# Attention with two gated layers on one core: the sums' guard on ScalarE, the first pair without GpSimd, small work with a choice of engine, and a new planned order

## The chip, the core and the metric

The kernel runs on one core of a Trainium2 chip. The metric is the device time of one execution in microseconds (us); what is compared is the median of several runs. Profiles are taken of one execution. The core has five engines that run side by side, each working through its own instructions in the order in which they were written: TensorE (PE in the profile; PEld is its weight load), VectorE (DVE), ScalarE (ACT), GpSimd (POOL) and SyncE (SP), which here issues nearly all transfers between memory and the core.

## The reference

```python
def _attn_ref(q, k, v):                     # q, k, v: 4 x 8 heads x 576 x 64
    q_rot, k_rot = (rotate(q), rotate(k))   # rotary embedding, cos and sin tables
    scores = scale * np.matmul(q_rot, k_rot.transpose(0, 1, 3, 2))
    scores = scores - np.max(scores, axis=-1, keepdims=True)
    attn = np.exp(scores)
    attn = attn / (np.sum(attn, axis=-1, keepdims=True) + 1e-09)
    return np.matmul(attn, v).astype(np.float32)

def _moe_ref(x, w_gate, w_val, w_out):      # 2304 tokens x 512, 1536 wide
    g = x @ w_gate
    silu = g * (1.0 / (1.0 + np.exp(-g)))
    return (silu * (x @ w_val) @ w_out).astype(np.float32)

def _moe2_ref(x, w_in, w_out):              # 2304 tokens x 512, 2048 wide
    r = np.maximum(x @ w_in, 0.0)
    return (r * r @ w_out).astype(np.float32)

# reference: _moe2_ref(_moe_ref(_attn_ref(q, k, v) as tokens x 512))
```

The `1e-09` that is added to the sums of the softmax is what the text calls the guard.

## The kernel before

The work falls into two stages. The first is attention, in 16 pairs of heads (4 blocks of the batch, 4 pairs each). The second holds the two gated layers and is one long run of matmuls. Each fp32 operand is split into a high and a low part in the fp32r format, and a product is made of three matmuls: high by high, high by low, low by high.

In the first stage nothing runs in the order in which it stands in the code. The functions `add_prep`, `add_kq`, `add_scores`, `add_values`, `add_spill`, `add_weight` and `add_filler` hand small operations to a `Plan`: the engine (or several to choose from, `add_any`), a time in ns that the planner takes for it, what it reads and writes, and a rank. `Plan.order()` then goes through a clock of its own: whenever an engine is free it takes the ready operation of lowest rank, and an operation with several engines goes to the first that takes it. The resulting order is written out, and each engine works through its share of it in that order, waiting on semaphores. The ranks come from the tables `RANK`, `RANK0` (first block) and `RANK1` (first two pairs); `FIRST` orders the first pair. `HOPS` holds times from engine to engine, `SWITCH` what a return of TensorE from transposes (mode 1) to products (mode 0) is taken to cost, `STAY` what is added to the rank of the other mode.

For each pair: q and k come in with the rotated halves beside them (tile `rot`); rope is a multiplication by the tables `cs` (or `csq`, which is `cs` times 0.125) and an addition of both halves (lines 487 and 488, on GpSimd, for pair 1 on GpSimd or VectorE). ScalarE makes the high part (line 531), GpSimd the low one (line 533), and SyncE copies both into the tiles `kh`, `qa` and `qz` by DMA (line 545). TensorE makes the scores `s` (line 565, two PSUM places), VectorE their maximum (571), ScalarE the exponential with its sum (573) into `p`. TensorE transposes `p` (594, two PSUM places `pt`), ScalarE or VectorE copies the result out (586, 588), TensorE multiplies by v (628, 631).

The sums are treated so: GpSimd adds the guard (line 637 for four columns, twice in a pair; line 600 for the ninth, once), VectorE takes the reciprocal (638, 601), ScalarE broadcasts it to `rb` (639), TensorE transposes `rb` (649) and VectorE multiplies (651). A normalised tile is split by ScalarE (657) and GpSimd (659). Pair 0 is different: rope on VectorE straight from the loads (481, 483), high parts by ScalarE (515, 521), low parts by VectorE (516, 522), and `qz` is a GpSimd copy of `qa` (525). The table `csq` is made by ScalarE (736).

Fillers are matmuls of the first gated layer for blocks 0 to 2 and its first two chunks of weights (line 704); they are planned into the attention stage with ranks of their own, and their weights are unpacked there (lines 226 to 231).

Of the kernel before, what the change touches and what calls it, by code (L numbers as in the profile page):

```python
# [12 lines left out]
AF = mybir.ActivationFunctionType  # L13
# [10 lines left out]
RANK0 = dict(ld=-0.835, rope=-50.984, k=29.955, lo=-87.1, dup=32.08, v=-8.825, s=-140.07, mx=-104.755, ex=-124.918, pt=-62.05, hi=246.519, av=23.841, rec=-40.109, x=-103.798, out=-29.73, fin=-99.107, scale=7.973)  # L24
RANK1 = dict(ld=53.997, rope=-27.634, k=14.826, lo=-66.302, dup=-17.819, v=-47.75, s=-62.932, mx=-81.823, ex=-200.205, pt=-33.078, hi=39.408, av=-5.906, rec=93.306, x=-80.138, out=-32.589, fin=-39.784, scale=-29.722)
# [22 lines left out]
class Plan:  # L48
# [9 lines left out]
    SWITCH = 80  # L58
    STAY = 67.654
# [4 lines left out]

    LAND = 2000
    RATE = 350

    def add(self, eng, ns, fn, rd=(), wr=(), rank=0.0, hold=0, mode=0, port=False, size=0, claim=()):
        self.add_any([(eng, ns, fn)], rd, wr, rank, hold, mode, port, size, claim)

    def add_any(self, ways, rd=(), wr=(), rank=0.0, hold=0, mode=0, port=False, size=0, claim=()):
# [18 lines left out]
        self.ops.append(dict(ways=ways, eng=ways[0][0], ns=ways[0][1], fn=ways[0][2], deps=deps, bufs=bufs, rank=(round(rank, 6), i), hold=hold, mode=mode, port=port, size=size))  # L90

    def order(self):
# [10 lines left out]
        busy, mode = {}, {}  # L103
        moved = 0.0
# [15 lines left out]
        out = []  # L120
        while events:
# [23 lines left out]
            for eng, heaps in ready.items():  # L145
                while any(heaps) and not busy.get(eng):
# [35 lines left out]
def tile_attention_moe_moe2(  # L182
# [161 lines left out]
    with ExitStack() as p1:  # L344
# [114 lines left out]
        def add_prep(g):  # L459
# [5 lines left out]
            for n, (c0, c1) in enumerate(parts(g)):  # L465
# [7 lines left out]
                for i in (1, 0):  # L473
                    x = P["rot"][i]
                    if g == 0:

                        at0 = FIRST["rope"][n][i]
                        y = buf("pt", [128, 512], bufs=2, pool=pp) if i else buf(("av", "mm")[n], [128, 512], pool=pp)
                        for e in range(2):
                            o = (lambda x=x, c0=c0, c1=c1: x()[:, 0, c0:c1]) if e == 0 else (lambda y=y, w=w: y()[:, :w])  # L480
                            plan.add("DVE", dve(w, 150), lambda x=x, o=o, c0=c0, c1=c1, e=e: nc.vector.tensor_tensor(out=o(), in0=x()[:, e, c0:c1], in1=cs()[:, e, c0:c1], op=ALU.mult),
                                     [(cs, n)] + ([] if e == 0 else [(x, n)]), [(x, n)] if e == 0 else [y], at0, port=True)
                        plan.add("DVE", dve(w, 150), lambda x=x, y=y, w=w, c0=c0, c1=c1: nc.vector.tensor_tensor(out=y()[:, :w], in0=y()[:, :w], in1=x()[:, 0, c0:c1], op=ALU.add), [(x, n)], [y], at0)
                        P[i, n] = (y, lambda y=y, w=w: y()[:, :w])
                        continue
# [4 lines left out]
                    for cols, fn in steps:  # L490
# [3 lines left out]
                        plan.add_any(ways, csk if i else [csq], [(x, n)], at + 0.01 * (1 - i), port=True)  # L494
# [6 lines left out]
        def add_kq(g):  # L501
# [5 lines left out]
            if g == 0:  # L507
                for n, (c0, c1) in enumerate(PARTS):
                    w, c = c1 - c0, slice(c0, c1)
                    (yk, kx), (yq, qx) = P[1, n], P[0, n]  # L510
                    for h in range(2):
                        own, other = rowsof(h)
                        at = FIRST["k"][n][h]
                        for r, p in ((own, 0), (other, 1)):
                            plan.add("ACT", act(w, 190), lambda h=h, own=own, r=r, c=c, kx=kx: nc.scalar.activation(kh()[r, h, c], kx()[own], AF.Copy), [yk], [(kh, (h, p, n))], at)
# [3 lines left out]
                        for (c, qc), (_, zc) in zip(q_at(h, c0, c1, NR), q_at(h, c0, c1, 0)):  # L519
# [5 lines left out]
                            plan.add("Pool", 550, lambda own=own, qc=qc, zc=zc: nc.gpsimd.tensor_copy(qz()[own, zc], raw(qa()[own, qc])), [(qa, (h, 0, n))], [(qz, (h, n))], at)  # L525
# [11 lines left out]
            for h in range(2):  # L537
# [6 lines left out]
                for (key, src), c, dst, wr, late in moves:  # L544
                    plan.add("SP", 450, lambda src=src, own=own, c=c, dst=dst: nc.sync.dma_start(out=raw(dst()), in_=src()[own, c]), [key], wr, at + 0.005 * late, size=256 * (c.stop - c.start))  # L545

        def add_scores(g):
# [4 lines left out]
            for x in range(NT):  # L552
# [3 lines left out]
                for i in range(2):  # L556
# [13 lines left out]
                    plan.add("PE", pe(HS) * (2 if t < 4 else 3), mm, rd, [ps], at + rk("s", g))  # L570
# [6 lines left out]
        def add_values(g):  # L577
# [22 lines left out]
            plan.add("Pool", 110, lambda: nc.gpsimd.tensor_scalar(rr(), sums()[:, 8:9], 1e-9, None, ALU.add), [(sums, 8)], [rr], at)  # L600
# [4 lines left out]
            for i in range(2):  # L605
# [3 lines left out]
                for c in range(5):  # L609
                    at = start + c * 0.08  # L610
                    pt = buf("pt", [128, 512], bufs=2, pool=pp)
                    plan.add("PE", 4 * 110, lambda c=c, pt=pt, tiles=tiles, pcs=pcs: (pcs[c](), transposes(tiles, c, pt, 0)), tiles, [pt], at + rk("pt", g), mode=1, claim=[pcs[c]])
                    copy(pt, pcs[c], 512, 128 if c < 4 else NR, at + rk("hi", g), [pcs[c]])
                rdr = []
                if i:
                    pcr = pcr_of()
                    for n in range(2):
                        at = start + (5 + n) * 0.08
                        pt = buf("pt", [128, 512], bufs=2, pool=pp)
                        plan.add("PE", (4 - 3 * n) * 110, lambda n=n, pt=pt, pcr=pcr: [pcr()] + [transposes([pr], c, pt, 128 * (c % 4)) for c in (range(4), (4,))[n]], [pr], [pt], at + rk("pt", g), mode=1, claim=[pcr])  # L620
# [11 lines left out]
                plan.add("PE", 5 * 420 + 300 + 600 * i, mm, pcs + rdr + [(vt, 0), (vt, 1)], [av], start + 0.45 + rk("av", g), mode=1)  # L632
# [265 lines left out]
```

## Time and profile before

| what | value |
|---|---|
| median of 3 runs | 1152.36 us (1151.9 to 1153.92) |
| the profiled execution | 1151.21 us, its span 1149.4 us |
| busy share of the span | TensorE 97%, VectorE 50%, ScalarE 42%, GpSimd 42% |
| chain that ended last, by engine | PE 77%, POOL 8%, DMA 5%, DVE 3%, SPq 2%, ACT 2%, issue 2% |
| mean granted clock of TensorE | 0.997 |

The span goes from the first to the last instruction of the profiled execution; the time of the run has a little more around it. A wait is given as the idle time of an engine in front of an instruction, with the instruction that ended the wait behind an arrow. A busy TensorE is not a TensorE at its peak, as matmuls overlap and their ends are modelled; what counts below is when it stood still.

### The profile page before, as it was taken

The numbers are of one execution on the slowest core, as the hardware profiler recorded it, in microseconds if no ns is written. First come the engines' busy times: TensorE is split into PE (matmuls) and PEld (weight loads), VectorE is DVE, ScalarE is ACT, GpSimd is POOL, SyncE is SP. The second block draws the span as 40 slices with busy tenths as digits, with TensorE's granted clock in tenths as the row PEclk, the third lists the DMA queues.
The fourth block names the chain that finished last, engine by engine and source line by source line (L and its number), as shares of the span: only waits on it lengthen the run. The fifth ranks groups of instructions, "written<-read, shape, count | busy, mean of one in ns | idle before, by whom it ended". The sixth has DMA issues, their size and how long they took to land.

```text
span 1149.4 us, 16627 instructions
## 1 busy us (share of the span) xinstructions
PE 1110.1 (97%) x6336; PEld 929.5 (81%) x6336; DVE 574.4 (50%) x953; ACT 477.6 (42%) x970; POOL 487.2 (42%) x417
## 2 busy tenths in 40 slices
PE   4898999999999999999999999999999999999998
PEld 3686877788888888888888888888888888888886
DVE  7676765766673655537346274461153236233222
ACT  6666766676663433213132132443352224223121
POOL 6887666576214433214132144562243234224121
PEclk9999999999999999999999999999999999999999
DMA  9765655646327522103011020120031012000112
GB/s 297 214 186 170 170 171 161 185 135 176 79 75 261 206 74 73 39 4 107 1 56 55 1 92 19 37 74 1 1 105 42 1 48 81 1 1 1 67 26 74
DMA packets 61104, 102.44 MB, mean 89 GB/s; under 512 B 11104, under 2 KB 37216, under 8 KB 60128
## 3 DMA queue, kind: packets, MB, share of 16 engines
q1 hardware_dynamic: 59904, 96.59, 28.0%
q0 software_dynamic: 576, 4.19, 1.0%
q8 instruction: 50, 0.82, 0.3%
q10 hardware_dynamic: 544, 0.59, 0.2%
q14 instruction: 30, 0.25, 0.1%
HBM read 67.17 MB, written 12.06 MB: 69 GB/s over the span
## 4 chain that ended last, share of the span: by engine, by line
PE 77%; POOL 8%; DMA 5%; DVE 3%; SPq 2%; ACT 2%; issue 2%; POOLq 0%; DVEq 0%; ACTq 0%
PE mm L267 22%; PE mm L268 22%; PE mm L269 22%; PE s L565 3%; PE pt L594 3%; POOL rot L487 3%; PE av L628 3%; PE mm L704 2%; SPq L545 2%; POOL rot L488 1%; DMA rot<-in_k_dram 1%; DMA qa<-rot 1%; DMA v<-in_v_dram 1%; DMA rot<-in_q_dram 1%; POOL kl L533 1%
## 5 line engine op out<-in xcount | busy, mean ns | idle before, releaser
L282 POOL TENSOR_TENSOR h<-s,h 128x512 fp32r<-128x512 f32 (+1 forms) x80 | 96.2, 1202 | 182.1 <-ACT h L281 182.1
L282 POOL TENSOR_TENSOR h<-hf,h 128x512 fp32r<-128x512 f32 (+1 forms) x54 | 66.8, 1237 | 151.6 <-ACT h L281 148.9
L301 DVE TENSOR_TENSOR s<-r,mm 128x512 f32<-128x512 f32 (+1 forms) x80 | 50.6, 632 | 147.0 <-POOL h L282 75.4
L571 DVE TENSOR_REDUCE nm<-s 128x1 f32<-128x576 f32 x144 | 104.6, 749 | 21.2 <-PE s L565 20.1
L573 ACT ACTIVATE p<-s,nm 128x576 f32<-128x576 f32 x144 | 105.7, 737 | 20.3 <-DVE nm L571 18.7
L565 PE MATMUL s<-kh,qa 128*128 128x288 f32 x320 | 94.0, 326 | 18.8 <-DVE qa L522 10.8
L594 PE MATMUL pt<-ident,p 128*128 128x128 f32 (+1 forms) x720 | 101.4, 279 | 10.4 <-DVE pc L588 6.6
L268 PE MATMUL mm<-wo,h 128*128 128x512 f32 x288 | 110.8, 389 | 0.0
L267 PE MATMUL mm<-wo,h 128*128 128x512 f32 x288 | 109.5, 389 | 0.0
L594 PEld LDWEIGHTS pt<-ident,p 128*128 128x128 f32 (+1 forms) x720 | 82.6, 137 | 23.4 <-DVE pc L588 8.4
L269 PE MATMUL mm<-wo,h 128*128 128x512 f32 x288 | 93.2, 389 | 0.0
L299 ACT ACTIVATE r<-mm 128x512 f32<-128x512 f32 (+1 forms) x80 | 43.9, 549 | 118.5 <-PE mm L269 118.1
L231 POOL TENSOR_TENSOR wi<-wa,wi 128x512 fp32r<-128x512 f32 x36 | 47.2, 1310 | 108.3 <-ACT wi L230 108.3
L290 DVE SCALAR_TENSOR_TENSOR th<-th,mm 128x512 f32<-128x512 f32 (+1 forms) x54 | 33.8, 626 | 107.2 <-ACT th L288 107.2
L565 PE MATMUL s<-kl,qz 128*128 128x288 f32 x288 | 83.0, 305 | 1.6 <-POOL qz L525 1.6
L228 DVE SCALAR_TENSOR_TENSOR wp<-wa,wp 128x512 uint32<-128x512 uint32 x62 | 53.4, 862 | 58.4 <-ACT wa L226 58.4
L565 PEld LDWEIGHTS s<-kh,qa 128*128 128x128 f32 x320 | 60.9, 196 | 25.9 <-ACT p L573 13.3
L281 ACT ACTIVATE h<-s 128x512 fp32r<-128x512 f32 (+1 forms) x80 | 47.2, 589 | 78.2 <-DVE s L301 78.2
L628 PE MATMUL av<-pc,v 128*64 128x256 f32 x640 | 76.8, 387 | 0.0
L269 PE MATMUL mm<-h,wo 128*128 128x512 f32 (+1 forms) x200 | 72.6, 369 | 0.0
L281 ACT ACTIVATE h<-hf 128x512 fp32r<-128x512 f32 (+1 forms) x54 | 31.5, 583 | 98.9 <-DVE hf L293 98.4
L268 PE MATMUL mm<-h,wo 128*128 128x512 f32 (+1 forms) x200 | 72.6, 368 | 0.0
(212 smaller groups left out, 2794.7 us busy)
## 6 DMA issues: line engine op xcount, KB each, us to landing
raw<-in_moe_w_out_dram SPq DMA_DIRECT2D x26, 512.0 KB, 3.5
rot<-in_k_dram SPq DMA_DIRECT2D x15, 576.0 KB, 4.2
rot<-in_q_dram SPq DMA_DIRECT2D x15, 576.0 KB, 3.8
kh<-rot SPq DMA_DIRECT2D x60, 144.0 KB, 2.6
raw<-in_moe_w_in_dram SPq DMA_DIRECT2D x16, 512.0 KB, 3.6
raw<-in_moe_w_gate_dram SPq DMA_DIRECT2D x10, 512.0 KB, 3.6
raw<-in_moe_w_val_dram SPq DMA_DIRECT2D x10, 512.0 KB, 3.7
qa<-rot SPq DMA_DIRECT2D x30, 144.0 KB, 2.6
```

Source lines behind the costliest of these rows:

```text
L228: lambda: nc.vector.scalar_tensor_tensor(out=p(), in0=a(), scalar=3, in1=p(), op0=ALU.logical_shift_left, op1=ALU.bitwise_or),
L267: nc.tensor.matmul(ps, lhsT=ah, rhs=bh, start=first, stop=False)
L268: nc.tensor.matmul(ps, lhsT=ah, rhs=bl, start=False, stop=False)
L269: nc.tensor.matmul(ps, lhsT=al, rhs=bh, start=False, stop=last)
L281: nc.scalar.activation(h[:, 0, :n], hf[:, :n], AF.Copy)
L282: nc.gpsimd.tensor_tensor(out=h[:, 1, :n], in0=hf[:, :n], in1=h[:, 0, :n].bitcast(F32), op=ALU.subtract)
L301: nc.vector.tensor_tensor(out=s[:, :n], in0=r[:, :n], in1=a, op=ALU.mult)
L565: nc.tensor.matmul(ps()[:, i, :HS], lhsT=a, rhs=w, start=y == 0, stop=y == len(prods) - 1)
L571: plan.add("DVE", 755, lambda ps=ps, nm=nm: nc.vector.tensor_reduce(out=nm(), in_=ps()[:, :, :HS], axis=AX.XY, op=ALU.max, negate=True), [ ...
L573: plan.add("ACT", 930, lambda x=x, ps=ps, nm=nm, p=p: nc.scalar.activation(p().rearrange("p (a b) -> p a b", a=2), ps()[:, :, :HS], AF.Exp ...
L594: nc.tensor.matmul(pt()[:kk, off + n * 128:off + n * 128 + 128], lhsT=p()[:, c * 128:c * 128 + kk], rhs=ident, is_transpose=True)
L628: nc.tensor.matmul(av()[h * 64:h * 64 + 64, 0:256], lhsT=vt()[:, h, c], rhs=pcs[c]()[:, h * 256:h * 256 + 256], start=c == 0, stop=c == 4)
```

## The change

- The guard of both kinds of sums is added by a ScalarE activation with a bias, where a GpSimd instruction did it.
- Pair 0: one VectorE multiplication takes both halves in place, and the addition reads both halves from SBUF. `qz` is written straight from the rotated q by ScalarE or VectorE, the copies into `kh` and the table `csq` may go to either of the two. One rope step on pair 1 names a tile of pair 0 as something that it reads.
- The broadcast of the reciprocals may go to ScalarE or GpSimd, the high part of the normalised tile to ScalarE or VectorE.
- The planner: all ranks are new (`FIRST` is not), `SWITCH` is 0 and `STAY` slightly negative, an issue of the copies into `kh`, `qa` and `qz` is taken at 590 ns and not at 450, and TensorE's operations carry a count of columns (`cols`), from which the planner takes TensorE at full or at half speed.

```diff
-RANK = dict(ld=176.169, rope=77.556, k=133.052, lo=-64.241, dup=130.669, v=-12.083, s=27.238, mx=100.534, ex=60.673, pt=-5.142, hi=45.754, av=95.071, rec=-6.745, x=179.568, out=-4.367, fin=-49.53, scale=-159.05, w=28.595, dw=27.25, fill=63.17, df=5.551)
+RANK = dict(csq=-22.67, ld=226.587, rope=115.785, k=115.695, lo=-117.099, dup=301.534, v=50.531, s=32.768, mx=120.695, ex=-3.238, pt=29.928, hi=32.2, av=122.763, rec=-50.518, x=196.241, out=62.378, fin=-121.67, scale=-103.611, w=-117.46, dw=116.396, fill=81.467, df=4.914)
...
-    SWITCH = 80
-    STAY = 67.654
+    SWITCH = 0
+    STAY = -3.043
...
+    TICK = 10240 / 3
+    COLUMNS = 3060
+    PHASE = 2190
...
+                    if eng == "PE":
+                        k = int((now + self.PHASE) / self.TICK)
+                        if k > tick:
+                            full = counted >= self.COLUMNS and k == tick + 1
+                            tick, counted = k, 0.0
+                        counted += ops[i]["cols"]
+                        ns *= 1 if full else 2
...
-                        for e in range(2):
-                            o = (lambda x=x, c0=c0, c1=c1: x()[:, 0, c0:c1]) if e == 0 else (lambda y=y, w=w: y()[:, :w])
...
+                        plan.add("DVE", dve(2 * w, 140), lambda x=x, c0=c0, c1=c1: nc.vector.tensor_tensor(out=x()[:, :, c0:c1], in0=x()[:, :, c0:c1], in1=cs()[:, :, c0:c1], op=ALU.mult),
+                                 [(cs, n)], [(x, n)], at0, port=True)
+                        plan.add("DVE", dve(w, 150), lambda x=x, y=y, w=w, c0=c0, c1=c1: nc.vector.tensor_tensor(out=y()[:, :w], in0=x()[:, 0, c0:c1], in1=x()[:, 1, c0:c1], op=ALU.add), [(x, n)], [y], at0, port=True)
...
-                            plan.add("ACT", act(w, 190), lambda h=h, own=own, r=r, c=c, kx=kx: nc.scalar.activation(kh()[r, h, c], kx()[own], AF.Copy), [yk], [(kh, (h, p, n))], at)
+                            ways = [("ACT", act(w, 190), lambda h=h, own=own, r=r, c=c, kx=kx: nc.scalar.activation(kh()[r, h, c], kx()[own], AF.Copy)),
+                                    ("DVE", dve(w, 150), lambda h=h, own=own, r=r, c=c, kx=kx: nc.vector.tensor_copy(kh()[r, h, c], kx()[own]))]
+                            plan.add_any(ways, [yk], [(kh, (h, p, n))], at + 0.01 * p)
...
-                            plan.add("Pool", 550, lambda own=own, qc=qc, zc=zc: nc.gpsimd.tensor_copy(qz()[own, zc], raw(qa()[own, qc])), [(qa, (h, 0, n))], [(qz, (h, n))], at)
+                            plan.add_any([("ACT", act(w, 190), lambda own=own, d=d, zc=zc, qx=qx: nc.scalar.activation(qz()[own, zc], qx()[own, d], AF.Copy, scale=0.125)),
+                                          ("DVE", dve(w, 150), lambda own=own, d=d, zc=zc, qx=qx: nc.vector.tensor_scalar(qz()[own, zc], qx()[own, d], 0.125, None, ALU.mult))],
+                                         [yq], [(qz, (h, n))], at + 0.01)
...
-                    plan.add("SP", 450, lambda src=src, own=own, c=c, dst=dst: nc.sync.dma_start(out=raw(dst()), in_=src()[own, c]), [key], wr, at + 0.005 * late, size=256 * (c.stop - c.start))
+                    plan.add("SP", 590, lambda src=src, own=own, c=c, dst=dst: nc.sync.dma_start(out=raw(dst()), in_=src()[own, c]), [key], wr, at + 0.005 * late, size=256 * (c.stop - c.start))
...
-            plan.add("Pool", 110, lambda: nc.gpsimd.tensor_scalar(rr(), sums()[:, 8:9], 1e-9, None, ALU.add), [(sums, 8)], [rr], at)
+            plan.add("ACT", 190, lambda: nc.scalar.activation(rr(), sums()[:, 8:9], AF.Copy, bias=1e-9), [(sums, 8)], [rr], at)
...
-                plan.add("Pool", 110, lambda i=i, rs=rs: nc.gpsimd.tensor_scalar(rs(), sums()[:, 4 * i:4 * i + 4], 1e-9, None, ALU.add), rd, [rs], at)
+                plan.add("ACT", 190, lambda i=i, rs=rs: nc.scalar.activation(rs(), sums()[:, 4 * i:4 * i + 4], AF.Copy, bias=1e-9), rd, [rs], at)
                 plan.add("DVE", 180, lambda rs=rs: nc.vector.reciprocal(out=rs(), in_=rs()), [], [rs], at)
-                plan.add("ACT", 411, lambda rs=rs, rb=rb: nc.scalar.activation(rb(), rs()[:, :, None].to_broadcast([128, 4, D]), AF.Copy), [rs], [rb], at)
+                plan.add_any([("ACT", 411, lambda rs=rs, rb=rb: nc.scalar.activation(rb(), rs()[:, :, None].to_broadcast([128, 4, D]), AF.Copy)),
+                              ("Pool", 700, lambda rs=rs, rb=rb: nc.gpsimd.tensor_copy(rb(), rs()[:, :, None].to_broadcast([128, 4, D])))], [rs], [rb], at)
...
-                plan.add("ACT", act(n_, 190), lambda xi=xi, sl=sl, src=src: nc.scalar.activation(xbuf[xi]()[0][:, j, sl], xs()[:, src], AF.Copy),
-                         rd, [(xbuf[xi], (0, g))], at)
+                plan.add_any([("ACT", act(n_, 190), lambda xi=xi, sl=sl, src=src: nc.scalar.activation(xbuf[xi]()[0][:, j, sl], xs()[:, src], AF.Copy)),
+                              ("DVE", dve(n_, 60), lambda xi=xi, sl=sl, src=src: nc.vector.tensor_copy(xbuf[xi]()[0][:, j, sl], xs()[:, src]))],
+                             rd, [(xbuf[xi], (0, g))], at, port=True)
...
-        plan.add("ACT", act(2 * S), lambda: nc.scalar.activation(csq(), cs(), AF.Copy, scale=0.125), csk + [(pair[0]["qa"], (1, 0, 1))], [csq], -900)
+        plan.add_any([("ACT", act(2 * S), lambda: nc.scalar.activation(csq(), cs(), AF.Copy, scale=0.125)),
+                      ("DVE", 700, lambda: nc.vector.tensor_scalar(csq(), cs(), 0.125, None, ALU.mult))], csk + [(pair[0]["qa"], (1, 0, 0))], [csq], rk("csq", 0), port=True)
```

## Rows read from the trace of the kernel before

**Rows 1.** The page's first part: busy us (share of the span) and instructions of each engine.

```profile
PE 1110.1 (97%) x6336; PEld 929.5 (81%) x6336; DVE 574.4 (50%) x953; ACT 477.6 (42%) x970; POOL 487.2 (42%) x417
```

**Rows 2.** Windows: length; busy us of PE, PEld, DVE, ACT, POOL; granted clock; DMA.

```profile
40.00:60.00 20.00, 15.94 (x132) 13.43 (x128) 14.25 (x27) 13.05 (x29) 16.03 (x14) 0.91 0.81 238
80.00:100.00 20.00, 17.92 (x145) 14.30 (x143) 11.86 (x21) 11.69 (x29) 13.71 (x12) 0.91 0.62 175
240.00:360.00 120.00, 118.94 (x955) 98.66 (x954) 72.18 (x135) 75.41 (x174) 47.67 (x54) 1.00 0.44 122
360.00:1150.00 790.00, 783.29 (x3746) 660.22 (x3744) 339.14 (x524) 245.60 (x436) 267.66 (x216) 1.00 0.17 53
```

**Rows 3.** TensorE's waits, whole span: waiter, who ended it: us in total, times, longest.

```profile
PE s L565 <- DVE qa L522: 10.8, 1, 10.8
PE s L565 <- ACT p L573: 7.7, 12, 2.4
PE pt L594 <- DVE pc L588: 6.6, 7, 3.5
PE pt L594 <- ACT pc L586: 3.3, 3, 2.1
PE pt L649 <- ACT pc L586: 1.8, 1, 1.8
```

**Rows 4.** Timeline of TensorE near 48 us: start, us, instruction, idle time before it.

```profile
48.69 0.66 PE L594 MATMUL pt<-ident,p 128*128 128x128 f32 x4 [3.54 <-DVE pc L588]
```

**Rows 5.** Timeline of GpSimd, 40 to 49 us.

```profile
44.93 2.61 POOL L487 TENSOR_TENSOR rot<-rot,csq 128x1152 f32<-128x1152 f32 x1 [3.23 <-issue]
47.62 0.22 POOL L637 TENSOR_SCALAR rs<-sums 128x4 f32<-128x4 f32 x1
```

**Rows 6.** Timeline of VectorE, 40 to 49 us.

```profile
47.88 0.18 DVE L638 RECIPROCAL rs<-rs 128x4 f32<-128x4 f32 x1 [3.79 <-POOL rs L637]
47.98 1.26 DVE L588 COPY pc<-pt 128x512 f32<-128x512 f32 x2
```

**Rows 7.** Timeline of TensorE at three later stalls.

```profile
150.28 0.44 PE L594 MATMUL pt<-ident,p 128*128 128x128 f32 x2 [2.07 <-ACT pc L586]
...
180.94 1.09 PE L594 MATMUL pt<-ident,p 128*128 128x128 f32 x5 [0.91 <-DVE pc L588]
...
202.87 0.40 PE L565 MATMUL s<-kh,qa 128*128 128x288 f32 x1 [1.09 <-ACT p L573]
```

**Rows 8.** Timeline of VectorE at the first and the last of these.

```profile
149.11 0.18 DVE L638 RECIPROCAL rs<-rs 128x4 f32<-128x4 f32 x1 [3.02 <-POOL rs L637]
...
201.11 0.18 DVE L638 RECIPROCAL rs<-rs 128x4 f32<-128x4 f32 x1 [2.19 <-POOL rs L637]
```

**Rows 9.** Waits of all engines, 0 to 420 us.

```profile
ACT rot L531 <- POOL rot L488: 30.1, 20, 4.6
DVE rs L638 <- POOL rs L637: 29.2, 16, 3.8
...
POOL rot L487 <- DMA qa<-rot: 20.2, 6, 6.4
...
DVE rr L601 <- POOL rr L600: 12.3, 11, 2.1
```

**Rows 10.** Groups by line and shape: ScalarE's accumulator reads, 0 to 360 us.

```profile
L573 ACT ACTIVATION_READ_ACCUMULATOR p<-s,nm 128x1 f32 x144 | 28.5, 198 | 0.0
```

**Rows 11.** Timeline of all engines, the first products of pair 0.

```profile
10.76 0.61 PE L565 MATMUL s<-kh,qa 128*128 128x288 f32 x1 [10.76 <-DVE qa L522]
...
12.23 1.13 POOL L525 CAST qz<-qa 64x288 fp32r<-64x288 f32 x2
...
12.93 0.61 PE L565 MATMUL s<-kl,qz 128*128 128x288 f32 x1 [1.57 <-POOL qz L525]
```

**Rows 12.** The same view: GpSimd's scaled product near 25 us, VectorE beside it.

```profile
23.94 1.49 DVE L488 TENSOR_TENSOR rot<-rot 128x576 f32<-128x576 f32 x1
...
24.77 3.16 POOL L487 TENSOR_TENSOR rot<-rot,csq 128x1152 f32<-128x1152 f32 x1
```

More of the change, by code (lines that the diff above doesn't have):

```diff
@@ L63, in __init__, with add, add_any @@
         self.ops = []
+    TICK = 10240 / 3
+    COLUMNS = 3060
+    PHASE = 2190
     LAND = 2000
     RATE = 350
-    def add(self, eng, ns, fn, rd=(), wr=(), rank=0.0, hold=0, mode=0, port=False, size=0, claim=()):
-        self.add_any([(eng, ns, fn)], rd, wr, rank, hold, mode, port, size, claim)
-    def add_any(self, ways, rd=(), wr=(), rank=0.0, hold=0, mode=0, port=False, size=0, claim=()):
+    def add(self, eng, ns, fn, rd=(), wr=(), rank=0.0, hold=0, mode=0, port=False, size=0, claim=(), cols=0):
+        self.add_any([(eng, ns, fn)], rd, wr, rank, hold, mode, port, size, claim, cols)
+    def add_any(self, ways, rd=(), wr=(), rank=0.0, hold=0, mode=0, port=False, size=0, claim=(), cols=0):
         i = len(self.ops)
@@ L89, in add_any @@
             buf.users += 1
-        self.ops.append(dict(ways=ways, eng=ways[0][0], ns=ways[0][1], fn=ways[0][2], deps=deps, bufs=bufs, rank=(round(rank, 6), i), hold=hold, mode=mode, port=port, size=size))
+        self.ops.append(dict(ways=ways, eng=ways[0][0], ns=ways[0][1], fn=ways[0][2], deps=deps, bufs=bufs, rank=(round(rank, 6), i), hold=hold, mode=mode, port=port, size=size, cols=cols))
     def order(self):
@@ L103, in order @@
         busy, mode = {}, {}
+        tick, counted, full = 0, 0.0, False
         moved = 0.0
@@ L493, in add_prep @@
                             ways.append(("DVE", dve(cols, 100), lambda fn=fn: fn(nc.vector)))
-                        plan.add_any(ways, csk if i else [csq], [(x, n)], at + 0.01 * (1 - i), port=True)
+                        plan.add_any(ways, (csk if i else [csq]) + ([pair[0][0, 1][0]] if g == 1 else []), [(x, n)], at + 0.01 * (1 - i), port=True)
             vt, s = P["v"], v[b, 2 * j:2 * j + 2]
@@ L569, in add_scores @@
                     rd += [(kh, (h_, y, i)) for h_ in hs_ for y in range(2)] + [(kl, (h_, i)) for h_ in range(2)]
-                    plan.add("PE", pe(HS) * (2 if t < 4 else 3), mm, rd, [ps], at + rk("s", g))
+                    plan.add("PE", pe(HS) * (2 if t < 4 else 3), mm, rd, [ps], at + rk("s", g), cols=HS * (2 if t < 4 else 3))
                 plan.add("DVE", 755, lambda ps=ps, nm=nm: nc.vector.tensor_reduce(
@@ L611, in add_values @@
                     pt = buf("pt", [128, 512], bufs=2, pool=pp)
-                    plan.add("PE", 4 * 110, lambda c=c, pt=pt, tiles=tiles, pcs=pcs: (pcs[c](), transposes(tiles, c, pt, 0)), tiles, [pt], at + rk("pt", g), mode=1, claim=[pcs[c]])
+                    plan.add("PE", 4 * 110, lambda c=c, pt=pt, tiles=tiles, pcs=pcs: (pcs[c](), transposes(tiles, c, pt, 0)), tiles, [pt], at + rk("pt", g), mode=1, claim=[pcs[c]], cols=1024)
                     copy(pt, pcs[c], 512, 128 if c < 4 else NR, at + rk("hi", g), [pcs[c]])
@@ L619, in add_values @@
                         pt = buf("pt", [128, 512], bufs=2, pool=pp)
-                        plan.add("PE", (4 - 3 * n) * 110, lambda n=n, pt=pt, pcr=pcr: [pcr()] + [transposes([pr], c, pt, 128 * (c % 4)) for c in (range(4), (4,))[n]], [pr], [pt], at + rk("pt", g), mode=1, claim=[pcr])
+                        plan.add("PE", (4 - 3 * n) * 110, lambda n=n, pt=pt, pcr=pcr: [pcr()] + [transposes([pr], c, pt, 128 * (c % 4)) for c in (range(4), (4,))[n]], [pr], [pt], at + rk("pt", g), mode=1, claim=[pcr], cols=1024 - 768 * n)
                         copy(pt, lambda n=n, pcr=pcr: pcr()[:, 512 * n:512 + 128 * n], 512 - 384 * n, 128 - 64 * n, at + rk("hi", g), [(pcr, n)])
@@ L649, in norm @@
                         nc.tensor.matmul(pt()[:, t * 128:t * 128 + 128], lhsT=rb()[:, 2 * t:2 * t + 2].rearrange("p a b -> p (a b)"), rhs=ident, is_transpose=True)
-                plan.add("PE", 220, norm, [rb, (xs, i)], [pt], at, mode=1)
+                plan.add("PE", 220, norm, [rb, (xs, i)], [pt], at, mode=1, cols=512)
                 plan.add("DVE", dve(256), lambda i=i, pt=pt: nc.vector.tensor_tensor(
@@ L703, in mms @@
                         plan.add("PE", pe(n), lambda x=x, y=y, f=(i == 0 and jj == 0), l=(i == len(wl) - 1 and jj == 2):
-                                 nc.tensor.matmul(ps()[:, :n], lhsT=x(), rhs=y(), start=f, stop=l), rd + (rdi[i] if rdi else []), [ps], rank[0])
+                                 nc.tensor.matmul(ps()[:, :n], lhsT=x(), rhs=y(), start=f, stop=l), rd + (rdi[i] if rdi else []), [ps], rank[0], cols=n)
             hs = []
```

9 lines of the change are left out of this document (3 added, 6 removed).

## The prediction

> **What bounds the kernel now.** The page's first part comes first: TensorE is busy for 1110.1 us of a span of 1149.4 [rows 1], so at most 39.3 us of the span are idle on it. The windows say where. From 360 us to the end TensorE is busy for 783.29 of 790 us, and what is missing there is nearly all the last store after the last matmul; from 240 to 360 it is busy for 118.94 of 120 [rows 2]. The change touches only the planned attention stage, which lies before 360 us, so some 790 us of the span stay as they are, and the question is what TensorE loses before. The list of TensorE's waits answers that: 10.8 us before the first product, then 7.7 behind softmax's exponentials, 6.6 and 3.3 behind the two engines that copy transposed tiles out of PSUM, 1.8 behind the same at another line [rows 3]; with five small entries of 3.1 us together the list comes to 33.3 us. The clock adds a little: the granted clock was 0.91 of full in 40 to 60 and again in 80 to 100 us [rows 2], which is about 3.6 us in each at 1.2 GHz in place of 2.4.
>
> The largest single wait behind a copy is worth following back. TensorE stood still for 3.54 us before 48.69 [rows 4], for a copy on VectorE. VectorE was free, but in its order of work a tiny reciprocal (line 638) stood ahead of that copy, and it waited 3.79 us for GpSimd; the copies started 0.1 us behind it [rows 6]. GpSimd's part is the guard of line 637, 0.22 us of work, and it stood behind a rope product of 2.61 us that itself began late [rows 5]. So 0.22 us of work on an engine that waits for loads stopped VectorE, and VectorE stopped TensorE. Three more of TensorE's waits end in the same way: 2.07 us before 150.28, 0.91 before 180.94, 1.09 before 202.87 [rows 7], each shortly behind a reciprocal on VectorE that GpSimd had released, the first at 149.11 and the last at 201.11 [rows 8]. Over the stage, 16 of 32 reciprocals for four columns and 11 of 16 for one waited for GpSimd, 29.2 and 12.3 us [rows 9]; most of that cost TensorE nothing, because its queue had other work.
>
> **The change part by part.** *The guard on ScalarE.* Forty-eight GpSimd instructions go, and 48 small ScalarE instructions come. The sums are written by ScalarE itself, so its guard can wait for no other engine's data; the reciprocal then waits only until ScalarE reaches the guard. What goes is 3.54 + 2.07 + 0.91 + 1.09 = 7.6 us of TensorE's idle time. Is something else late in those places? At 48.69 the tiles that TensorE wanted copied were in PSUM already, and the copies follow the reciprocal at once [rows 6], so nothing else held them; I take 7.6 whole, with 0 as the other end (another wait there just as long). The slow clock of 40 to 60 us follows that stall; TensorE was otherwise dense before and after it. With the stall gone I take the slow stretch to go too: 3.6 us of work at 1.2 GHz shrink to 1.8, so 1.8 us (0 at the other end).
>
> The price of the 48 on ScalarE: the nearest row is its read of an accumulator, one column, 198 ns [rows 10], so 48 x 0.2 = 9.6 us. ScalarE is busy for 75.41 of 120 us in 240 to 360 [rows 2], so most of it fits in gaps; but ahead of an exponential or a copy it delays them, and TensorE waits behind ScalarE for 7.7 + 3.3 + 1.8 = 12.8 us as it is [rows 3]. I take a tenth, +1.0 us, with 0 and one half (+4.8) as the ends. What it queues behind: any ScalarE instruction in front, above all the copy of line 531, which waits for GpSimd's rope (second rival).
>
> *The first pair without GpSimd.* Before, the second product of the first tile stood 1.57 us for a GpSimd cast of qz [rows 11], and that cast began at 12.23 only because GpSimd had a rope product in front. Now ScalarE or VectorE writes qz straight from PSUM, and GpSimd is off this path. Against that, five or six more pieces of about 0.4 us land on the two engines that carry the chain from the first load to the first exponential. The two rope multiplications of a part become one of twice the columns with the same element count, so nearly nothing moves there. The first product at 10.76 [rows 11] is held by loads and by that chain, not by GpSimd. Ends: 1.6 us gained, 1.0 lost (two or three pieces in the way). I take 1.0 gained, nearer to the row.
>
> *Work free to go to either engine.* Broadcast of the reciprocals (ScalarE or GpSimd), split of the normalised tile, first copies, scaled table (ScalarE or VectorE). All of it has an engine with a third of its time free in rows 2, so I cost it at nothing; it hides behind the exponentials and TensorE's own work. If that cover is gone it is in the ScalarE term above. Broadcasts that go to GpSimd leave ScalarE's queue, and bring a GpSimd wait back in front of a normalising TensorE instruction, which is a bound of its own: GpSimd waited up to 6.4 us for a store into qa [rows 9], 3.4 us on average in six such waits. One of these in front of TensorE would cost 3.4.
>
> On GpSimd and VectorE together the trace shows one thing that speaks against the change: the rope product at 24.77, beside an addition on VectorE that reads two halves of a tile in SBUF and takes 1.49, took 3.16 us [rows 12] where the one at 44.93 took 2.61 [rows 5], half a us more. The Trainium skill, GPSIMD Engine Reference, section Key points, says that GpSimd shares its SBUF interfaces with VectorE and meets contention from VectorE instructions in a two-port mode or with two SBUF inputs; the new addition of the first pair and the new VectorE ways are of that sort. By that rule the two new additions that fall beside GpSimd's first rope product would draw out the first pair by up to half a us, and the time would be 1143.5 and not 1143.0. GpSimd itself has the time to spare (47.67 of 120 us busy, rows 2), so my sum holds no term for such meetings.
>
> *The order planned anew.* Every rank changes, a return from transposes to products is now costed at nothing, stores at 590 ns each, and the planner doubles TensorE's times in stretches where it takes the clock to be low. Nothing in the trace gives a price for another order. What it can touch is the rest of TensorE's waits: 33.3 - 10.8 - 7.6 = 14.9 us. I take 0, with half of it either way (7.5) as ends.
>
> The sum: 7.6 + 1.8 + 1.0 - 1.0 = 9.4 us of gain. The profiled execution took 1151.21 us in all, 1.81 more than its span; less 9.4 that is 1141.8, span 1140.0. The median of the three runs, 1152.36, lies 1.15 above the profiled run, so the median to expect is 1143.0.
>
> **The rivals.** *Deeper gain.* The new order also takes away the waits behind ScalarE's line 531 and the exponentials. For it: the 1.80 us in front of line 649 [rows 3] and the second stretch of low clock [rows 2] have that look, and half of the 14.9 us plus 1.8 of clock are there to be had. Against it: nothing in the diff aims at them but ranks. 1143.0 - 7.5 - 1.8 = about 1134.
>
> *The wait moves to ScalarE (slower).* Line 531 on ScalarE waited for GpSimd's rope 20 times, 30.1 us in all, up to 4.6 [rows 9]: 1.5 us each. Today such a wait stops ScalarE's copies only, VectorE takes the others, and TensorE shows one of 1.80 us. If the plan puts guards behind line 531, the reciprocal on VectorE waits as well, both copying engines stand, and TensorE stands for the whole 1.5 us. It decides from six such places: 6 x 1.5 = 9.0 us eats the gain. With twelve, 18 us go, and 1143.0 + 18 = 1161. For it: GpSimd's rope is late for reasons that an order on ScalarE doesn't see, as the 20.2 us that it waits for stores into qa show [rows 9]. Against it: the guard is ready long before its reciprocal is needed, and its rank puts it early.
>
> *Refilled.* TensorE's gaps close at the guard and open elsewhere, since the pace of a pair is set by exponentials and maxima of ScalarE and VectorE; the 7.6 us come back as waits for the exponentials, of which there are 7.7 us now [rows 3], and the clock stays as it is. Then 1152.4 - 1.0 + 1.0, about 1152, no change. For it: twelve waits of TensorE end with an exponential now, more than with anything else [rows 3]. Against it: the three stalls after 150 us [rows 7] come where the windows show TensorE nearly full, so other work is at hand there.
>
> **How the numbers follow.** Forecast 0.52, deeper gain 0.14, refilled 0.14, moved to ScalarE 0.20. No change means within 0.2% (2.3 us), about what a measurement of this kernel can tell from none: 1150.1 to 1154.7. Faster 0.66, same 0.14, slower 0.20. The bounds of the terms give 7.6 + 1.8 + 1.6 + 7.5 = 18.5 us of gain at the good end, 1134; at the other, 0 + 0 - 1.0 - 4.8 - 7.5, which is 13 us slower, 1166, but not all at once. The range goes from 1134 to 1156: it takes in the refilled case and the beginning of the slower one, and leaves out perhaps 0.07 below and 0.13 above. The forecast's own range is 1137 to 1150.
>
> **What would show it.** Right: no reciprocal on VectorE waits for GpSimd, and those that wait for ScalarE sum to a few us; TensorE's waits fall from 33.3 to about 25; the windows of 40 to 60 us show the full clock; the second product of the first tile follows the first within 1 us. Wrong: reciprocals wait for ScalarE, released by line 531's end; TensorE's normalising products wait for GpSimd's broadcasts; waits for exponentials grow beyond 12 us; or the stretch behind 360 us changes its length, which I take as fixed.

## The result and the profile after

The median of the changed kernel is 1141.51 us (1141.16 to 1142.10, 4 runs), that of the kernel before 1152.13 in the same runs: a ratio of 0.9905, 95% interval 0.9888 to 0.9922, or 10.9 us less by the ratio (10.6 between the medians). The forecast was 1143.0. The profiled execution took 1142.10 us, its span 1140.3.

The page's first part, busy us of each engine, against rows 1:

```profile
PE 1105.8 (97%) x6336; PEld 927.6 (81%) x6336; DVE 593.9 (52%) x978; ACT 473.2 (41%) x983; POOL 480.1 (42%) x375
```

The same number of matmuls keeps TensorE busy 4.3 us less, and it is idle for 34.5 us where it was 39.3. The waits of TensorE, whole span, against rows 3 (waiter, who ended it, us in total, times, longest):

```profile
PE s L578 <- DVE qa L533: 12.1, 1, 12.1
PE s L578 <- ACT p L586: 10.7, 9, 3.1
PE s L578 <- DMA qz<-rot: 2.3, 2, 1.6
PE pt L607 <- ACT pc L599: 1.7, 3, 1.2
PE pt L663 <- ACT pc L599: 1.0, 1, 1.0
PE mm L278 <- DVE xs L665: 0.7, 1, 0.7
```

No wait for VectorE's copies is left (6.6 us before), those for ScalarE's copies went from 5.1 to 2.7. The first product comes later (12.1 for 10.8), and the waits for exponentials grew from 7.7 to 10.7. The whole list comes to 28.5 us, where it came to 33.3. The windows, against rows 2 (length; busy us of PE, PEld, DVE, ACT, POOL; granted clock; DMA):

```profile
40.00:60.00 20.00, 18.47 (x153) 14.74 (x154) 17.27 (x31) 17.03 (x44) 18.14 (x13) 1.00 0.73 215
80.00:100.00 20.00, 16.50 (x151) 13.42 (x149) 12.04 (x22) 12.66 (x32) 12.83 (x8) 1.00 0.69 185
240.00:360.00 120.00, 118.77 (x937) 98.63 (x936) 78.53 (x142) 69.43 (x165) 45.37 (x41) 1.00 0.45 140
360.00:1141.00 781.00, 774.75 (x3703) 653.17 (x3701) 333.73 (x517) 241.41 (x429) 263.24 (x213) 1.00 0.15 49
```

Both stretches of low clock are gone, though TensorE stands still for longer in 80 to 100 us than it did. The last window has 6.2 us idle of 781; before it was 6.7 of 790. It is shorter because it starts at a fixed time and the attention stage now ends sooner: the first matmul of the long gated run (line 278, line 267 of before) began at 346.24 us and not at 354.55, and from there to the end the span has 794.1 us where it had 794.9. So 8.3 of the 9.1 us between the two spans lie in the attention stage. What the guard was to change shows among all waits up to 420 us, against rows 9:

```profile
ACT rot L544 <- POOL rot L497: 23.4, 13, 3.6
...
DVE rs L651 <- ACT rs L650: 3.8, 4, 1.2
```

The reciprocals of four columns wait for ScalarE 3.8 us in all, where they waited 29.2 for GpSimd. Line 544 is 531 of before: ScalarE's wait for the rope stays.

### The profile page after: what moved, and what is told of

The parts are those of the page before. It is cut to its first block, busy times and chain, and to the rows that moved or that the text cites. A ratio compares the mean times of both kernels' runs of the same rounds, so it can differ in the third digit from the quotient of the medians.

```text
span 1140.3 us, 16604 instructions
## 1 busy us (share of the span) xinstructions
PE 1105.8 (97%) x6336; PEld 927.6 (81%) x6336; DVE 593.9 (52%) x978; ACT 473.2 (41%) x983; POOL 480.1 (42%) x375
## 4 chain that ended last, share of the span: by engine, by line
PE 81%; DMA 1%; ACT 0%; DVE 0%; SPq 0%; issue 0%; DVEq 0%
PE mm L278 23%; PE mm L279 23%; PE mm L280 23%; PE s L578 3%; PE pt L607 3%; PE av L641 3%; PE mm L719 3%; DMA kh<-rot 0%; PE av L644 0%; DMA rot<-in_q_dram 0%; PE pt L663 0%; DMA qa<-rot 0%; DMA out_dram<-zs 0%; ACT p L586 0%; SPq L558 0%; DVE zs L846 0%
## 5 line engine op out<-in xcount | busy, mean ns | idle before, releaser
L578 PE MATMUL s<-kh,qa 128*128 128x288 f32 x320 | 101.4, 344 | 25.5 <-DVE qa L533 12.1
L607 PE MATMUL pt<-ident,p 128*128 128x128 f32 (+1 forms) x720 | 107.0, 275 | 1.8 <-ACT pc L599 1.7
L607 PEld LDWEIGHTS pt<-ident,p 128*128 128x128 f32 (+1 forms) x720 | 85.2, 135 | 9.4 <-ACT pc L599 2.8
L578 PEld LDWEIGHTS s<-kh,qa 128*128 128x128 f32 x320 | 60.1, 194 | 37.7 <-ACT p L586 17.6
L601 DVE COPY pc<-pt 128x512 f32<-128x512 f32 (+1 forms) x98 | 65.9, 684 | 19.1 <-PE pt L607 18.2
```

Source lines behind the costliest of these rows:

```text
L578: nc.tensor.matmul(ps()[:, i, :HS], lhsT=a, rhs=w, start=y == 0, stop=y == len(prods) - 1)
L601: nc.vector.tensor_copy(dst()[:kk], pt()[:kk, :n])
L607: nc.tensor.matmul(pt()[:kk, off + n * 128:off + n * 128 + 128], lhsT=p()[:, c * 128:c * 128 + kk], rhs=ident, is_transpose=True)
```

## Experiments

Each group ran beside the kernel before, on one chip; its medians there lay at 1153.2, 1152.9 and 1153.8 us, so ratios are compared, and a difference in us is the ratio's part of 1152. "In its order" means that only the emitted instruction was changed and the planner saw the old one, so every other instruction kept its place.

**The guard alone**, in the order of before:

```diff
-lambda i=i, rs=rs: nc.gpsimd.tensor_scalar(rs(), sums()[:, 4 * i:4 * i + 4], 1e-9, None, ALU.add)
+lambda i=i, rs=rs: nc.scalar.activation(rs(), sums()[:, 4 * i:4 * i + 4], AF.Copy, bias=1e-9)
```

(and line 600 likewise)

> The kernel before with nothing changed but the engine of the 48 guards: ScalarE in place of GpSimd, each at the same place of the same order. Theory 'guard': the four stalls of TensorE behind the reciprocals (7.6 us) and the slow clock after the first of them (1.8) go, some 1 us comes for ScalarE's time: 1143 to 1146 us, and no reciprocal waits for GpSimd. Theory 'order': the guard alone is worth under 3 us, because other waits of the old order take its place: 1149 to 1152 us. Theory 'moved to ScalarE': guards behind line 531 keep the stalls, 1152 us or more, with the reciprocals waiting for ScalarE.

Measured 1150.12, ratio 0.9969 (0.9958 to 0.9981): 3.6 us less, under half of the 8.4 us that the prediction's terms give it (7.6 + 1.8 - 1.0), and within the range of theory 'order'. TensorE's timeline, then ScalarE's, then one row of GpSimd's show why:

```profile
47.96 0.63 PE L594 MATMUL pt<-ident,p 128*64 128x128 f32 x4 [1.01 <-DVE pc L588]
51.36 0.40 PE L565 MATMUL s<-kh,qa 128*128 128x288 f32 x1 [2.78 <-ACT p L573]
...
151.55 0.84 PE L594 MATMUL pt<-ident,p 128*64 128x128 f32 x3 [2.13 <-ACT pc L586]
```

```profile
49.42 0.68 ACT L531 ACTIVATE rot<-rot 128x576 fp32r<-128x576 f32 x1 [4.07 <-POOL rot L488]
50.01 0.58 ACT L586 ACTIVATE pc<-pt 128x512 f32<-128x512 f32 x1
...
149.81 0.68 ACT L531 ACTIVATE rot<-rot 128x576 fp32r<-128x576 f32 x1 [2.99 <-DMA rot<-in_q_dram]
...
193.73 0.68 ACT L531 ACTIVATE rot<-rot 128x576 fp32r<-128x576 f32 x1 [4.22 <-POOL rot L488]
```

```profile
148.35 1.42 POOL L488 TENSOR_TENSOR rot<-rot 128x576 f32<-128x576 f32 x1
```

The stall of 3.54 us before 48.69 shrank to 1.01, but TensorE then stood 2.78 us a little later; that of 2.07 before 150.28 came back as 2.13. These two now end with ScalarE, whose exponentials and copies stood behind line 531, which waited for the rope (at 149.81 the profile names a load, but the rope's addition on GpSimd ended at 149.77). And the clock, in the same kernel's windows:

```profile
80.00:100.00 20.00, 17.64 (x143) 14.20 (x142) 12.10 (x21) 11.68 (x31) 12.56 (x8) 0.91 0.60 174
140.00:160.00 20.00, 17.87 (x135) 14.96 (x136) 13.12 (x23) 13.25 (x34) 13.87 (x10) 0.91 0.54 154
190.00:210.00 20.00, 17.46 (x115) 14.13 (x114) 11.51 (x23) 12.11 (x30) 11.98 (x8) 0.91 0.58 161
```

With a further stretch near 53 us it fell to 1.2 GHz four times in this profile, where the profile of before shows two. Over all executions of this group the two kernels lie close together: the mean granted clock was 0.994 with the guard alone and 0.995 before.

**The guard back on GpSimd**, in the new order (the reverse of the diff above):

> The changed kernel with the 48 guards back on GpSimd, each at the same place of the new order. Theory 'guard': what was gained there is lost again, 1147 to 1151 us, reciprocals wait for GpSimd for over 20 us. Theory 'order': the new order is what gained, and the guard's engine matters for under 2 us: 1141 to 1143.5 us.

Measured 1154.31, ratio 1.0007 (0.9995 to 1.0019): the whole gain is gone, more than either theory said. A wait of TensorE and one of VectorE that came back:

```profile
PE pt L607 <- DVE pc L601: 7.0, 5, 3.9
```

```profile
DVE rs L651 <- POOL rs L650: 26.8, 15, 5.0
```

The old pattern is back with the old sizes (6.6 us and 29.2 us before). TensorE's waits rose from 28.5 to 35.3 us, which is 6.8 of the 12; its busy time rose as well, from 1105.8 to 1111.1, with one stretch of low clock between 120 and 140 us (0.91). So the guard on ScalarE is worth 3.6 us in the old order and some 12 in the new: the new order can't do without it, and the guard alone doesn't gain the whole in the old one.

**The old ranks for the new operations** (old `RANK`, `RANK0`, `RANK1`, `SWITCH`, `STAY`, 450 ns for a store, no clock):

```diff
-                        ns *= 1 if full else 2
+                        pass
```

> The changed operations (guard on ScalarE, pair 0 without GpSimd, both-way work), but ordered with the ranks of before, the old SWITCH and STAY, the old price of a store, and TensorE always at full speed in the planner. Theory 'guard': as good as the changed kernel within 3 us, 1140 to 1145 us. Theory 'order': most of the gain is gone, 1148 to 1154 us. In between, 1145 to 1148, both count.

Measured 1154.76, ratio 1.0013 (1.0003 to 1.0024): nothing gained. In this order the changed operations are no gain by themselves; it is one order, and the next runs show how far one order can be from another.

**The clock in the planner.** First the changed kernel with the one line of the last diff, all ranks new:

> The changed kernel, new ranks, but the planner takes TensorE at full speed throughout. Theory 'the clock in the planner matters': TensorE's stretches at 1.2 GHz come back and the time rises by over 2.5 us, to 1144 or more. Theory 'it doesn't': within 2 us of the changed kernel, 1139.5 to 1143.5.

Measured 1153.97, ratio 1.0002 (0.9989 to 1.0016). That looked like the clock. But any change of the planner gives another order, so three more orders were made with the same operations and ranks: two with the clock, one without it.

```diff
-    HOP = 200
+    HOP = 210
```

> The changed kernel with its new ranks and with the clock in the planner; only the planner's general time from engine to engine is 210 ns and not 200, which gives another order. Theory 'the clock in the planner is what gains': as good as the changed kernel, under 1144 us. Theory 'the ranks are fitted to one order': any other order loses most of the gain, 1147 to 1155 us, like the run without the clock (1.0002 of before).

Measured 1155.20, ratio 1.0016 (1.0003 to 1.0029).

```diff
-    RATE = 350
+    RATE = 340
```

> As the run before, with the planner's rate of transfers at 340 and not 350 bytes per ns in place of the other change; a second order with the clock. Theory 'clock in the planner': under 1144 us. Theory 'fitted ranks': 1147 to 1155 us.

Measured 1169.56, ratio 1.0138 (1.0121 to 1.0155).

```diff
-    HOP = 200
+    HOP = 210
...
-                        ns *= 1 if full else 2
+                        pass
```

> The changed kernel without the clock in the planner (as one run before) and with 210 ns from engine to engine: a second order without the clock. Theory 'clock in the planner': 1149 to 1156 us, like the first such run, and over 4 us above both orders with the clock. Theory 'fitted ranks': anything from 1145 to 1156, not apart from the two orders with the clock.

Measured 1157.91, ratio 1.0037 (1.0021 to 1.0054). Without the clock two orders gave 1.0002 and 1.0037, with it 1.0016, 1.0138 and the changed kernel's 0.9905. The clock in the planner doesn't set them apart; the ranks fit one order, and 5% of one general constant loses all of it. In the slowest of them part of the loss is at the end of the stage. TensorE's waits there:

```profile
PE pt L607 <- ACT pc L599: 6.8, 5, 3.1
PE mm L278 <- ACT ys L746: 4.2, 1, 4.2
PE mm L719 <- ACT ys L746: 2.4, 2, 1.7
```

The last two are filler results that were left over, with ScalarE's copies of them (line 746) in a row behind one PSUM place.

**Pair 0's addition from PSUM**, in the new order:

```diff
-tensor_tensor(out=x()[:, :, c0:c1], in0=x()[:, :, c0:c1], in1=cs()[:, :, c0:c1], op=ALU.mult)
+tensor_tensor(out=x()[:, 0, c0:c1], in0=x()[:, 0, c0:c1], in1=cs()[:, 0, c0:c1], op=ALU.mult)
+tensor_tensor(out=y()[:, :w], in0=x()[:, 1, c0:c1], in1=cs()[:, 1, c0:c1], op=ALU.mult)
-tensor_tensor(out=y()[:, :w], in0=x()[:, 0, c0:c1], in1=x()[:, 1, c0:c1], op=ALU.add)
+tensor_tensor(out=y()[:, :w], in0=y()[:, :w], in1=x()[:, 0, c0:c1], op=ALU.add)
```

> The changed kernel, in its order, with pair 0's rope as before: two VectorE multiplications of 288 columns, the second into PSUM, and an addition that reads PSUM and SBUF. Theory 'shared interface': the addition of the last quarter of pair 0, which took 2.10 us beside a GpSimd product in the changed kernel, falls under 0.6 us, TensorE's wait of 2.96 us before its third tile shrinks by over 1 us, and the time falls by 1 to 3 us, to 1138.5 to 1140.5. Rival 'the start has slack': the addition falls but the time stays within 1 us of 1141.5, as later tiles wait for something else.

Measured 1145.88, ratio 0.9935 (0.9916 to 0.9954): some 3.5 us slower than the changed kernel (the two intervals meet at their ends), so both theories missed. What was to be mended is this, in the changed kernel, VectorE and then GpSimd:

```profile
14.93 2.10 DVE L492 TENSOR_TENSOR mm<-rot 128x288 f32<-128x288 f32 x1
16.95 0.75 DVE L584 TENSOR_REDUCE nm<-s 128x1 f32<-128x576 f32 x1
```

```profile
13.77 2.93 POOL L496 TENSOR_TENSOR rot<-rot,csq 128x1152 f32<-128x1152 f32 x1 [1.60 <-ACT csq L751]
```

In the experiment the addition did shrink, but the second multiplication, which also reads two tiles of SBUF, now fell beside the same product. VectorE, then GpSimd:

```profile
14.22 2.89 DVE L490 TENSOR_TENSOR mm<-rot,cs 128x288 f32<-128x288 f32 x1
```

```profile
14.15 2.63 POOL L496 TENSOR_TENSOR rot<-rot,csq 128x1152 f32<-128x1152 f32 x1 [1.80 <-ACT csq L751]
```

In both kernels the VectorE instruction ended 0.33 us behind GpSimd's (14.93 + 2.10 and 13.77 + 2.93; 14.22 + 2.89 and 14.15 + 2.63). It was not slowed by a share, it was held until GpSimd was done. The tile that the expectations here and below call the third is the fourth: in the changed kernel it began at 20.21, the third at 15.93.

The 3.5 us are not in TensorE's waits: these come to 28.5 us in both kernels, the start included. TensorE was busy for 1109.1 us and not 1105.8, and its clock was low twice, where the changed kernel has 1.00 in the same windows:

```profile
80.00:120.00 40.00, 36.43 (x303) 30.27 (x303) 27.15 (x48) 27.06 (x67) 26.05 (x17) 0.96 0.69 185
180.00:200.00 20.00, 18.23 (x142) 14.75 (x141) 10.87 (x22) 10.97 (x28) 11.02 (x7) 0.91 0.62 183
```

By these rows the clock cost 0.04 x 40 + 0.09 x 20 = 3.4 us, about the whole difference (an estimate). Why it fell in this order and not in the other isn't shown.

**The split of the normalised tile always on ScalarE**, in the new order (line 672's `nc.vector.tensor_copy` emitted as the activation of line 671):

> The changed kernel, in its order, with the high part of the normalised tile always on ScalarE (17 of 32 were on VectorE, where copies of 512 columns took between 0.48 and 1.65 us). Theory 'shared interface costs time there as well': VectorE is freed of some 15 us and the time falls by over 1.5 us, to 1140 or less. Rival 'off the path': within 1.5 us of 1141.5; or slower, up to 1145, as ScalarE's queue is the tighter one.

Measured 1143.39, ratio 0.9909 (0.9891 to 0.9927), the changed kernel's own. VectorE's busy time fell from 593.9 to 579.1 us, as reckoned, and it was worth nothing: either this work is off the path, or ScalarE paid for it as much. The 17 pieces show the same hold in the changed kernel. By shape (count, busy us, mean ns) they differ widely, and the timeline of VectorE and then of GpSimd shows one of them:

```profile
L672 DVE CAST x2h<-xs 128x512 fp32r<-128x512 f32 x4 | 4.7, 1166 | 0.1
...
L672 DVE CAST x3h<-xs 128x512 fp32r<-128x512 f32 x4 | 1.9, 480 | 0.1
```

```profile
127.64 1.65 DVE L672 CAST x1h<-xs 128x512 fp32r<-128x512 f32 x1
```

```profile
127.59 1.41 POOL L497 TENSOR_TENSOR rot<-rot 128x576 f32<-128x576 f32 x1
```

It ended 0.29 us behind GpSimd's addition. Twelve of the 17 are 512 columns wide. All eight of these that began while a GpSimd instruction of two inputs had over 0.2 us to go ended 0.28 or 0.29 us behind it; the other four took 0.41 to 0.43.

**The high copies on GpSimd**, in the new order:

```diff
-lambda x=x: nc.scalar.activation(high(x), x()[:, 0], AF.Copy)
+lambda x=x: nc.gpsimd.tensor_copy(high(x), x()[:, 0])
```

> The changed kernel, in its order, with the 30 copies that make the high parts (line 544 there, 531 before) made by GpSimd and not by ScalarE, so that ScalarE never waits for GpSimd's rope. Theory 'ScalarE's queue stands behind GpSimd': TensorE's stalls before 97.3, 145.5, 166.8 and 188.1 us (6.9 us in all) go, and the time falls to 1134 to 1138. Rival 'GpSimd is the bound': the 30 copies of about 0.9 us make its rope later, stores into qa and kh land later, and the time is 1141 to 1150, with TensorE waiting for those stores.

In the changed kernel the largest stall left behind the start was this, TensorE and then ScalarE:

```profile
97.26 0.40 PE L578 MATMUL s<-kh,qa 128*128 128x288 f32 x1 [3.12 <-ACT p L586]
```

```profile
95.80 0.68 ACT L544 ACTIVATE rot<-rot 128x576 fp32r<-128x576 f32 x1 [3.33 <-POOL rot L497]
```

Measured 1139.27, ratio 0.9876 (0.9861 to 0.9891): 3.3 us less than the changed kernel, a little short of the expected. TensorE's waits with it:

```profile
PE s L578 <- DVE qa L533: 12.5, 1, 12.5
PE s L578 <- ACT p L586: 6.1, 7, 3.0
PE mm L719 <- POOL x0l L674: 2.7, 1, 2.7
PE s L578 <- DMA qz<-rot: 1.8, 1, 1.8
PE pt L607 <- ACT pc L599: 1.5, 2, 1.3
```

The four stalls (6.9 us) went; a wait of 2.7 us for GpSimd's low part came, with one stretch of low clock behind it (100 to 120 us, 0.91). GpSimd made a copy in 0.67 us.

**The guard and the high copies**, both in the order of before:

> The kernel before, in its order, with the guards on ScalarE (as in the run with the guard alone, 1150.1 us) and the 30 high copies of line 531 on GpSimd as well. Theory 'the stalls moved from the guard to line 531': the waits of 2.78, 2.08, 1.08, 2.13 and 2.54 us before 51.4, 88.6, 129.2, 151.5 and 195.0 us go with most of their slow clock, some 10 us and up to 6 of clock: 1136 to 1142 us. Rival 'another wait stands as long': 1147 us or more.

Measured 1143.50, ratio 0.9912 (0.9897 to 0.9928), between the ranges of the two theories: 6.6 us less than with the guard alone, in the old order and with nothing else of the change. TensorE's waits for ScalarE went from 17.6 us in the run with the guard alone to 5.9, while waits of 5.4 us for GpSimd's low parts (line 659) came. So most of what the guard alone lacked had gone to line 531; part of the 6.6 us may come from ScalarE being rid of the copies' own time. The high copies without the guard were not run, so what they gain by themselves isn't known.

**The table on VectorE**, on top of the high copies: the scaled table made right behind pair 0's last addition.

```diff
+nc.vector.tensor_scalar(csq(), cs(), 0.125, None, ALU.mult)   # behind the addition of q's second half
-nc.scalar.activation(csq(), cs(), AF.Copy, scale=0.125)
```

> The kernel with the high copies on GpSimd (1139.3 us), and the scaled table csq made by VectorE right behind pair 0's last rope addition, where ScalarE made it earlier: GpSimd's product that reads it can no longer run beside that addition. Theory 'shared interface': the addition falls from 2.1 us to under 0.6, TensorE's wait before its third tile (2.95 us) shrinks by over 1 us, and the time falls by 1 to 2 us, to 1137.3 to 1138.3. Rival 'pair 1 binds': the product begins some 2.4 us later, the stores for pair 1 land later, TensorE's 1.8 us wait for them near 36 us grows as much, and the time is 1139 or more.

Measured 1138.38, ratio 0.9868 (0.9852 to 0.9884): the lowest of all. Against the run without it that is 0.9 us, a little short of the 1 to 2 expected, and the intervals overlap, so the time alone doesn't show a gain. The trace does at the start: the addition fell from 2.10 to 0.46 us, TensorE's wait before the fourth tile from 2.95 to 1.98, and pair 1's scores began at 34.74 us and not at 35.97. VectorE, then TensorE:

```profile
15.14 0.46 DVE L492 TENSOR_TENSOR mm<-rot 128x288 f32<-128x288 f32 x1
15.51 0.75 DVE L492 TENSOR_SCALAR csq<-cs 128x1152 f32<-128x1152 f32 x1
```

```profile
19.45 0.61 PE L578 MATMUL s<-kh,qa 128*128 128x288 f32 x1 [1.98 <-ACT p L586]
```

## Why the forecast came out, and which of its steps didn't

The sum was 9.4 us and 10.9 were measured, but by other terms than the forecast's. The mechanism of the guard was right where it was looked for; that the number came so near is luck in good part, since two terms that were too large or of the wrong sign were made up for by the order, taken at 0, and by the clock, taken too small. Of the prediction's signs, the reciprocals, the full clock and the second product came as written; TensorE's waits fell to 28.5 us and not to about 25. The stretch behind 360 us did change its length, which was to speak against the forecast, but only because a stage that ends sooner leaves less behind a fixed time.

- **The guard, 7.6 us: too large as a term of its own.** In the changed kernel the four stalls of rows 4 and 7 are gone and the reciprocals wait as foreseen. Alone the guard gave 3.6 us, its clock and its price included. The step that failed is "nothing else held them; I take 7.6 whole". Something did, twice: ScalarE behind line 531. That was the rival "the wait moves to ScalarE", only that the reciprocals, which the rival put there, waited little (6.9 us for four columns and 7.2 for one, where they had waited 29.2 and 12.3 for GpSimd); ScalarE's own work was enough.
- **The clock, 1.8 us.** The step took the slow stretch to go with its stall. In the changed kernel both stretches went (20 us at a mean of 0.91 of full each [rows 2], 1.8 us short of it, so some 3.6 us given back between the two profiles), in the profile with the guard alone there were four. The clock followed the stalls that the order left, not the one stall removed. And the profile of before (0.997) was one of its executions with the higher clock: over the 49 executions of before that ran beside the experiments the mean granted clock was 0.995 (0.992 to 0.998), over the four of the changed kernel 0.9995. So the clock gave perhaps 2 to 5 of the 10.9 us. This is an estimate: 0.0045 of 1152 us is 5.2, while among the 49 those at 0.993 took 1154.3 us on average and those at 0.998 1151.9, which is 2.4 us for 0.005.
- **ScalarE's price, +1.0 us.** The guards took 205 and 198 ns where 200 were reckoned. Their share of the path was not measured by itself.
- **Pair 0, a gain of 1.0 us: the wrong sign.** The wait for qz went (1.57 us), but the first product came at 12.12 and not at 10.76, the fourth tile at 20.21 behind a wait of 2.96 where it had been 18.47, and pair 1's scores at 35.19, behind a wait of 1.60 for a store into qz, where they had been at 32.95. The products of a tile, 0.24 us apart at the start, came 0.13 apart from 27.9 us on, where they had done so from 25.9. The extra pieces and one held addition cost some 2 us.
- **The meeting of VectorE and GpSimd: at most half a us was set beside the sum; it was 1.64** (2.10 against 0.46). By the Trainium skill, GPSIMD Engine Reference, section Key points, VectorE instructions with two SBUF inputs contend with GpSimd; the trace agrees, and more sharply than it was read: the instruction that comes second is held until the first is done. The error was to price the meeting by GpSimd's loss (0.55 us) and not by VectorE's. The price stood in the row that the prediction read: its addition took 1.49 us [rows 12], but the same addition took 0.76 by itself, and the one of rows 12 had begun while an earlier product ran until 24.81. VectorE, then GpSimd, in the kernel before:

```profile
13.71 0.76 DVE L488 TENSOR_TENSOR rot<-rot 128x576 f32<-128x576 f32 x1
```

```profile
22.17 2.64 POOL L487 TENSOR_TENSOR rot<-rot,cs 128x1152 f32<-128x1152 f32 x1
```

- **The order, 0 with 7.5 either way: the largest term.** By difference it is worth about 9 us here (10.9 less 3.6, plus the 2 lost in pair 0), the clock's part included. That holds with the guard in place only: with the guard back on GpSimd the new order gained nothing (1.0007). Between five orders of the same operations and ranks the time varied by 27 us (0.9905 to 1.0138). The bounds were drawn from the waits that TensorE's list shows; but its busy time moved as well, from 1105.8 to 1110.0 and 1116.4 us in the changed kernel and the two other orders with the clock, and a list of waits has none of that. The lower clock explains some 1.8 us for each 20 us window at 0.91; the rest of that difference stays open.
- **Returns from transposes.** Counted in the sequence of TensorE's matmuls (with the products by v, which the planner puts in the same mode) they went from 100 to 208, and TensorE was busy for 4.3 us less than before, of which the clock explains 3.6. So no cost is seen, though no run changed these returns alone.

Of the rivals, "deeper gain" pointed at the right place: the waits behind line 531 were there to be had, but this change left most of them (ScalarE still waited 23.4 us of 30.1), and it took another edit. What in the new order makes it good isn't settled. No experiment took single ranks apart.

## What to carry to other kernels

In an engine's fixed order, a tiny instruction that waits for a slower engine stops all that stands behind it; before pricing its removal, look for the next instruction on the same copying engines that waits for the same source, since the first gain may move there (3.6 us for the guard, 10.1 with the high copies as well). A planned order with tuned ranks is one draw from a wide spread: to learn what an operation is worth, change the emitted instruction and keep the order, and test a planner's idea with several orders, not one.

## What the runs showed of the hardware

A VectorE addition or multiplication of two SBUF tiles that began while a GpSimd product ran ended 0.32 or 0.33 us behind that product in the three cases looked at, whether it had begun 1.16 us behind the product's start (2.10 us long), 0.07 (2.89) or, in the kernel before, 2.24 (begun at 11.90, 0.70 long, the product from 9.66 to 12.28); undisturbed it took 0.46. It goes the other way too: a GpSimd product that began while such a VectorE instruction ran was the one that lost, 0.3 us behind the multiplication begun at 13.46 in the changed kernel and 0.5 in rows 12.
